# Routing three batches of attention output in two lanes, with the rank in planned free steps of its PSUM bank

## The chip, the cores and the metric

The kernel runs on one core of one Trainium2 chip. The metric is the device time of one execution in microseconds (us), lower is better. Five engines work in parallel, each through its own instructions in order: PE (TensorE, matmuls; PEld are its weight loads), DVE (VectorE), ACT (ScalarE), POOL (GpSimd) and SP (SyncE, which here only issues DMAs). ACT and POOL also issue DMAs from their own queues.

## The reference

Three layers follow each other: attention with a threshold, a mixture of eight experts with one expert for each token, and a dense layer with softplus.

```python
# attention: batch 4, heads 8, seq 576, head_dim 64
scores = scale * q @ k.T
scores = where(scores >= max(scores) - tau, scores, -1e9)
attn = exp(scores - max(scores)); attn /= attn.sum() + 1e-9
x = (attn @ v) -> tokens x 512                    # 2304 x 512
# experts: 8, 512 -> 1024 -> 512
logits = (x / |x|) @ (emb / |emb|).T / tau
idx = argmax(logits); gate = softmax(logits)[idx]
out[n] = gate[n] * (relu(x[n] @ w1[idx[n]]) @ w2[idx[n]])
# dense: 512 -> 2048 -> 512
y = softplus(out @ w_in) @ w_out
```

## The kernel before, in words

The program is written under a manual schedule: each engine runs its instructions in the order in which the code emits them. It has three stages: attention (phase A, to about 380 us), experts (phase B, to about 660 us) and the dense layer (phase C, to the end).

Phase A works on 144 chunks (`NCH`), 36 for each of four batches: a chunk is 128 query rows of one head (or 64 rows of two heads). A step of the loop emits one chunk of scores on PE (`emit_s`, L314), their maximum and mask on DVE (`emit_max` L324, `emit_mask` L329), the exponentials on ACT (`emit_exp`, L340) and, some steps behind, the split of older chunks into two half floats (`emit_hi` on ACT, L354; `emit_lo` on POOL, tile `PST`), their transposition (by DMA from SP's queue, and a part on PE into the tile `T`, which ACT or DVE copy out in `emit_land`, L387 and L389) and the product with V (`emit_pv`, L412), ten steps behind the scores. DVE then scales the product into the rows `xs` (L428 to L438). What is emitted where is set by a list of (time, function): `at(n, ...)` puts a function near the end of step n, `soon(t, ...)` at a time t. Step n starts at the DVE instruction L324 of chunk n.

After the list comes the drain, whose order is written out as words (`DRAIN`): a letter and a number name a chunk function, or let one of the lanes take a step (z is lane 0, a lane 1, b lane 2).

Beside the chunks each step does a part of two slower jobs:

- **V of the next batch.** It is loaded in four pieces (`load_v`, from ACT's queue, into the one buffer `vst`), its greatest magnitude is found (`max_v`, ACT, L238), this is turned and spread by PE (`prep_v0`, `prep_vb`) and scaled on DVE (`prep_v1`, `prep_vc`, L256 to L277), and then V is scaled and rounded on ACT (`prep_v2`, L286 and L288, one head every second step) with the remainder on POOL (`prep_v3`, tile `vl`). `V0, VD, VM, VMD, VP` say at which step of a batch these parts stand.
- **Routing of the batch before.** For each 128 tokens, `route_sq` sums squares (ACT, L452), `route_t` transposes the rows on PE into a PSUM tile `xt_ps` (L460), `route_x` copies it out on ACT (L470), `route_l` makes the logits on PE (L481) and `route_c` copies them on DVE (L486). When the five pieces of a batch are there, generators do the rest, one small instruction at each half step: `route_norm` (the norm's reciprocal), `route_pick` (greatest logit, choice `eq`, `im`, one-hot `oh`), `route_gate` (softmax weight), `route_rank` (each token's place in its expert's bucket: matmuls L565 into a PSUM tile `rk_ps`, then `eq` L569 and `ix` L577 on DVE, the running counts `runs` on POOL) and `route_out` (five indirect DMAs on POOL, L615, that scatter the rows `xs` to the DRAM table `bucket`).

The PSUM tiles of V's chain (`vx_ps`, `vb_ps`), `xt_ps`, `lg_ps` and `rk_ps` are all cut from one pool `pr` with the tag `xt` and one buffer: a single bank. Whoever comes next on PE waits until the last user's copy has been read. The list `held` marks, while the program is being emitted, that a logits tile or a tile of V's chain is in use; `route_t` does not enter itself there.

Phase B starts with `counts` (tokens for each expert), loads of weights and of the first expert's rows from `bucket` (`load_x`, SP's queue, behind all scatters), 40 small matmuls, a branch on the overflow of a bucket (`overflow`), 40 more matmuls (`warm_up`, L1092), the gate's product with the rows (`gate_x`) and their transposition (`turn_first`, tile `x_ps`, L951) before the first expert matmul (L980).

Of the kernel before, what the change touches and what calls it, by code (L numbers as in the profile page):

```python
# [20 lines left out]
B, H, S, HD = 4, 8, 576, 64  # L21
# [13 lines left out]
PLAG = 5  # L35
WARMB, WARMC = 40, 40
TX0, TX = 4, 2
RKY, RKZ, VM, VMD = 2, 3, 17, 2
RKN, SUN, SU0 = 4, 0, 12
SBB, GQB, PTB = 6, 4, 4  # L40
LGL, LGZ, RNL, RSZ = 4, 3, 2, 3
C0 = NCH - 18
# [1 line left out]
OUTY = 2  # L44
EVA, EVH = 0, 0
DRAIN = """P8 g0 a1 z1 l2 a1 H2 a1 a1 H1 D3 a1 t5 P7 P6 a1 t4 D1 u5 L2 t3 a1 P5 c2 z1 p0 b1 V9 b1 a1 u4 a1 u3 P4 b1 t1 V5 b1 z1 b1 u1 t2 a1 u2 a1 z1 b1 z1 z1 a1 P3 r3 b1 b1 a1 x3 q3 b1 P2 V3 a1 b1 a1 g1 d1 d1 a1 P1 V1 l3 d1 r4 g2 d1 c3 q4 p1 d1 x4 d1 e1 f1 d1 e1 l4 f1 d1 e1 f1 e1 f1 d1 f1 e1 c4 z1 d1 e1 p2 h1 d1 e1 f1 d1 e1 f1 h1 a1 d1 e1 f1 h1 d1 f1 h1 f1 h1 f1 h1 d1 e1 d1 e1 e1 f1 h1 h1 e1 f1 d1 e1 f1 d1 e1 h1 d1 f1 f1 h1 e1 d1 d1 h1 d1 h1 e1 d1 e1 f1 h1 d1 e1 f1 h1 h1 e1 f1 f1 h1 d1 f1 h1 d1 e1 f1 e1 e1 f1 d1 f1 d1 e1 d1 h1 e1 h1 b1 h1 a1 z1 b1 z1 f1 b1 h1 a1 z1 b1 e1 e1 e1 b1 a1 a1 a1 d1 e1 b1 e1 d1 d1 e1 d1 e1 d1 d1 e1 d1 d1"""
QK0, QKD, V0, VD, VP, VS, Z0, ZD = 12, 7, 14, 2, 26, 2, 12, 1.5
DQ, DZ, VG = (0, 0, 0, 0), 1, 1
VA, VC, VE, VF = (1, 2, 3, 4), (3, 5), (5, 6, 7, 8, 9, 10, 11, 12), 1
NRING, L2LAG, CLAG, RAWB = 4, 2, 3, 3  # L50
# [11 lines left out]
def attention_moe_moe_kernel(ctx: ExitStack, tc, qT, kT, v, tau, emb, moe_tau, w1, w2, wi, wo, out):  # L62
# [121 lines left out]
    def phase_a():  # L184
        with ExitStack() as es:
# [359 lines left out]
            def route_rank(b, t0, t1, eq, oh, shift):  # L545
                T, R = t1 - t0, 64 if t0 == 4 else 128
                if T > 1:
                    sm1 = ry.tile([128, NE], F32, tag="sm1", name="sm1")[0:R]
                    dve.tensor_reduce(out=sm1, in_=oh.rearrange("p t e -> p e t"), axis=AX.X, op=ALU.add)
                    yield  # L550
                else:
                    shift()
                    IX[b, t0] = None
                    sm1 = oh[:, 0]
                    yield
                if b == B - 1 and t0 > 0:
                    pt = ps.tile([128, 2, 512], F32, tag="S", name="rk_ps")
                else:
                    while held:
                        yield  # L560
                    pt = pr.tile([128, 1, 512], F32, tag="xt", name="rk_ps")
                for t in range(T):
                    mms = ([(tri[0:R], oh[:, t]), (ones, runs)] + [(ones[0:R], oh[:, u]) for u in range(t)])
                    for z, (l, r) in enumerate(mms):
                        pe.matmul(pt[:, 0, t * NE:(t + 1) * NE], l, r, start=(z == 0), stop=(z == len(mms) - 1))  # L565
                if b == B - 1:
                    dve.tensor_tensor(out=runs[0:R], in0=runs[0:R], in1=sm1, op=ALU.add)
                    yield
                dve.tensor_tensor(out=eq, in0=pt[0:R, 0, 0:T * NE].rearrange("p (t e) -> p t e", t=T), in1=oh,  # L569
                                  op=ALU.mult)  # L570
                yield
                if b < B - 1:
                    combine(pool, runs[0:R], runs[0:R], sm1, ALU.add)
                    yield
                ix = sm.tile([128, 5], I32, tag="ix", name="ix")[0:R, 0:T]
                with nc.allow_low_precision(reason="whole numbers under 2**24"):
                    dve.tensor_reduce(out=ix, in_=eq, axis=AX.X, op=ALU.add)  # L577
                yield
                IX[b, t0] = ix
# [42 lines left out]
                    for _ in range(OUTY):  # L622
                        yield

            def route(b, t0, t1):
                yield from route_norm(b, t0, t1)
                for _ in range(RKN):
                    yield
                picked = yield from route_pick(b, t0, t1)
                yield from route_gate(b, t0, t1)  # L630
                for _ in range(RKY if b < B - 1 else 0):
                    yield
                yield from route_rank(b, t0, t1, *picked)
                yield from route_out(b, t0, t1)

            def route_p(b, t0, t1):
                picked = yield from route_pick(b, t0, t1)
                yield from route_rank(b, t0, t1, *picked)

            def route_g(b, t0, t1):  # L640
                yield from route_norm(b, t0, t1)
                while (b, t0) not in IX:
                    yield
                yield from route_gate(b, t0, t1)
                while IX[b, t0] is None:
                    yield
                for _ in route_out(b, t0, t1):
                    pass

            UT = {}  # L650

# [19 lines left out]
            def step_lane(k, n=1):  # L671
                q = lanes[k]
                for _ in range(n):
                    while q:
                        try:
# [2 lines left out]
                        except StopIteration:  # L678
                            q.pop(0)

            def step_tiny(n=0):
                for k in range(len(lanes)):
                    step_lane(k, TS if n > NFAST else 1)

# [34 lines left out]
            def at(n, fn, *a):  # L719
                work.setdefault(n, []).append((fn, a))  # L720
# [3 lines left out]
            def soon(t, fn, *a):  # L724
                late.append((t, fn, a))
# [26 lines left out]
            at(SU0, push, setup(em, ident16, pr, rt))  # L752
            for b in range(B):
                s0 = 36 * b
                for j in range(4):
                    at(s0 + QK0 + QKD * j, load_k, b + 1, j)
                    at(s0 + QK0 + QKD * j + 3, scale_k, b + 1, j)
                    at(s0 + QK0 + QKD * j + 2, load_q, b + 1, j)
                    at(s0 + V0 + VD * j, load_v, b + 1, 2 * j)
                    at(s0 + VM + VMD * j, max_v, b + 1, j)  # L760
                soon(s0 + VP + 0.05, prep_v0, b + 1)
                soon(s0 + VP + 1.18, prep_v1, b + 1)
                soon(s0 + VP + 2.85, prep_vb, b + 1)
                soon(s0 + VP + 3.18, prep_vc, b + 1)
                for i in range(0, 8, VN):
                    at(s0 + VP + 4 + VS * i, prep_v2, b + 1, i, VN)
                    at(s0 + VP + 5 + VS * i, prep_v3, b + 1, i, VN)
                    if (i + VN) % 2 == 0:
                        at(s0 + VP + 4 + VG + VS * i, prep_v4, b + 1, i + VN - 2, 2)
                for t in range(5 if b < B - 1 else 2):  # L770
                    s1 = pv_step[s0 + 8 * t + (7 if t < 4 else 3)] + (3 if b < B - 1 else RSZ)
                    at(s1, route_sq, b, t)
                    at(s1 + 1, route_t, b, t)
                    at(s1 + 1, route_x, b, t)
                    lg = LGL if b < B - 1 else LGZ
                    at(s1 + lg, route_l, b, t)
                    soon(s1 + lg + 1.19, route_c, b, t)
                    if t == 4:
                        at(s1 + RNL, push, route(b, 0, 5))
            for fn in (route_sq, route_t, route_x):  # L780
                at(NCH - 2, fn, B - 1, 2)
            for e in range(NE):
# [570 lines left out]
```

## Time and profile before

| | |
|---|---|
| median of 3 runs | 1097.32 us (1090.73 to 1097.51) |
| profiled execution | 1093.78 us, of which its span is 1092.1 us |
| PE / PEld busy | 978.2 / 834.6 us (90% / 76% of the span) |
| DVE / ACT / POOL busy | 713.8 / 609.2 / 560.6 us |
| mean granted TensorE clock | 0.959 |

The page of the profile gives, for one execution, each engine's busy time, the span in 40 slices, and the chain that ended last. A view of windows gives the same by stretch. A timeline lists instructions by start, with the idle time of that engine just before each and what released it. Busy shares are averages over stages with different limits, so each stage is read for itself.

### The profile page before, as it was taken

To read this page: it belongs to the slowest core of one execution; us is meant where nothing else is said; L and a number is where in the kernel's file an instruction comes from. 1 tells how busy PE (TensorE), PEld (TensorE's weight loads), DVE (VectorE), ACT (ScalarE), POOL (GpSimd) and SP (SyncE) were. 2 spreads that over 40 slices of the span, in tenths; PEclk is the share of its full clock that TensorE was granted. 3 is DMA by queue.
4 is the path that set the end of the run, shared out by engine and by line. 5 is a ranking of instruction groups with operands and counts; after the bars stand their busy time and mean duration, and the time that the engine had idled before them with its cause. 6 is when DMAs were issued, how large, how long until landed. Compare 5 with 4: busy or idle time off the path is not lost. (4 is left out here: it accounts for less than half of the span.)

```text
span 1092.1 us, 18861 instructions
## 1 busy us (share of the span) xinstructions
PE 978.2 (90%) x7110; PEld 834.6 (76%) x7110; DVE 713.8 (65%) x1393; ACT 609.2 (56%) x1070; POOL 560.6 (51%) x477
## 2 busy tenths in 40 slices
PE   7777986988888779989999988987999999999997
PEld 5566765766666769988998887765888888889896
DVE  7878897788689637666776658888433533444543
ACT  6769888788778525444444434445444544454543
POOL 4646665766766425544654431221655565565652
PEclk8889999899899879999999999999999999999999
DMA  6789997697667466978778775220200110010000
GB/s 161 157 152 180 181 222 133 135 187 127 138 105 112 134 223 194 220 157 192 208 231 196 167 180 135 91 87 20 77 1 1 30 39 1 29 40 1 29 1 30
DMA packets 181956, 128.39 MB, mean 118 GB/s; under 512 B 128856, under 2 KB 154456, under 8 KB 181856
## 3 DMA queue, kind: packets, MB, share of 16 engines
q1 hardware_dynamic: 162912, 99.84, 42.4%
q10 hardware_dynamic: 16032, 17.78, 6.1%
q0 software_dynamic: 2912, 9.48, 2.3%
q8 instruction: 58, 0.95, 0.4%
q14 instruction: 42, 0.34, 0.1%
HBM read 75.05 MB, written 20.01 MB: 87 GB/s over the span
## 5 line engine op out<-in xcount | busy, mean ns | idle before, releaser
L84 POOL TENSOR_TENSOR PST<-E,PST 128x1152 f16<-128x1152 f32 (+1 forms) x74 | 169.1, 2287 | 117.4 <-ACT PST L354 80.3
L1233 PE MATMUL a<-wo,g 128*128 128x512 f32 x864 | 218.4, 399 | 9.5 <-DVE g L84 9.5
L1205 PE MATMUL ch_ps<-cxt,wi 128*128 128x512 f32 (+1 forms) x960 | 214.3, 372 | 5.2 <-DVE cxt L84 3.2
L1205 PEld LDWEIGHTS ch_ps<-cxt,wi 128*128 128x128 f32 x960 | 177.2, 189 | 34.4 <-DVE cxt L84 3.5
L1233 PEld LDWEIGHTS a<-wo,g 128*128 128x128 f32 x864 | 162.1, 189 | 49.2 <-DVE g L84 14.0
L84 POOL TENSOR_TENSOR t<-e,t 128x512 f32<-128x512 f32 (+1 forms) x78 | 92.6, 1187 | 203.5 <-DVE t L1217 203.5
L314 PE MATMUL S<-k,qz 128*128 128x288 f32 x512 | 166.2, 451 | 8.7 <-ACT k L216 3.5
L324 DVE TENSOR_SCALAR_CACHE_REDUCE Sb<-S,tau_s 128x576 f32<-128x576 f32 x144 | 116.7, 810 | 46.5 <-PE S L314 36.8
L980 PE MATMUL h_ps<-xt,w 128*128 128x320 f32 x768 | 133.2, 323 | 12.7 <-ACT w L839 8.3
L84 POOL TENSOR_TENSOR w<-st,w 128x1024 fp32r<-128x1024 f32 x30 | 74.5, 2482 | 121.8 <-ACT w L839 121.6
L1217 DVE TENSOR_SCALAR t<-e 128x512 f32<-128x512 f32 (+1 forms) x80 | 33.6, 421 | 157.5 <-ACT e L1215 157.5
L980 PEld LDWEIGHTS h_ps<-xt,w 128*128 128x128 f32 x768 | 118.5, 195 | 18.2 <-ACT w L839 9.9
L1214 ACT ACTIVATE e<-ch_ps 128x512 f32<-128x512 f32 (+1 forms) x80 | 44.1, 551 | 154.1 <-PE ch_ps L1205 154.1
L996 PE MATMUL y<-h,w 128*128 128x320 f32 x768 | 123.0, 310 | 0.0
L329 DVE SCALAR_TENSOR_TENSOR Sb<-S,th,Sb 128x576 f32<-128x576 f32 x144 | 117.8, 818 | 5.1
L996 PEld LDWEIGHTS y<-h,w 128*128 128x128 f32 x768 | 115.7, 189 | 0.0
L314 PEld LDWEIGHTS S<-k,qz 128*128 128x128 f32 x512 | 93.8, 204 | 27.8 <-issue 5.0
L412 PEld LDWEIGHTS <-PT 128*128 128x128 f16 (+1 forms) x2240 | 87.2, 103 | 28.8 <-DMA PT<-PST 10.3
L340 ACT ACTIVATE E<-Sb,nb 128x576 f32<-128x576 f32 x144 | 103.8, 768 | 6.4 <-ACT nb L337 0.4
L412 PE MATMUL pv<-vh,PT 128*128 128x65 f16 (+1 forms) x1440 | 96.0, 197 | 10.8 <-DMA PT<-PST 7.5
L84 POOL TENSOR_TENSOR g<-g,t 128x512 f32<-128x512 f32 (+1 forms) x62 | 87.0, 1404 | 4.9
L839 ACT ACTIVATE w<-st 128x1024 fp32r<-128x1024 f32 x64 | 67.3, 1053 | 31.9 <-DMA st<-in_w 29.6
(185 smaller groups left out, 1377.1 us busy)
## 6 DMA issues: line engine op xcount, KB each, us to landing
st<-in_w SPq DMA_DIRECT2D x64, 512.0 KB, 4.8
raw<-in_wi SPq DMA_DIRECT2D x16, 512.0 KB, 4.2
raw<-in_wo SPq DMA_DIRECT2D x16, 512.0 KB, 5.4
bucket<-qz SPq DMA_DIRECT2D x32, 161.2 KB, 5.8
yT<-y ACTq DMA_DIRECT2D x7, 640.0 KB, 11.9
vst<-in_v ACTq DMA_DIRECT2D x12, 320.0 KB, 4.8
xr<-bucket SPq DMA_DIRECT2D x7, 516.0 KB, 6.3
k<-in_kT ACTq DMA_DIRECT2D x12, 288.0 KB, 4.0
```

Of the source, the lines that this page charges most:

```text
L84: eng.tensor_tensor(out=out, in0=a, in1=b, op=op)
L314: pe.matmul(st[:, f, 0:HALF], q[:, h // 2, o:o + 128], k[:, h // 2, fs])
L324: dve.tensor_scalar(out=Sb[n], in0=St[n][:, :, 0:HALF], scalar1=tau_s[:, 0:1], scalar2=None, op0=ALU.subtract, op1=ALU.max, accum_out=TH[g ...
L329: dve.scalar_tensor_tensor(out=Sb[n], in0=St.pop(n)[:, :, 0:HALF], scalar=TH[g][:, j:j + 1], in1=Sb[n], op0=ALU.is_lt, op1=ALU.subtract)
L340: act.activation(out=Et[g][:, i].rearrange("p (f k) -> p f k", f=2), in_=Sb.pop(g * GS + i), func=ACTF.Exp, scale=-SCALE, bias=nb[:, i:i + 1])
L412: pe.matmul(oo, l, r, start=(z == 0), stop=(z == len(mms) - 1))
L839: act.activation(out=hi, in_=src, func=ACTF.Copy)
L980: pe.matmul(hps[:, 0:CAP], a[:, c, 128 * (f % 2):128 * (f % 2) + 128], b[:, c], start=(z == 0), stop=(z == 11))
L996: pe.matmul(Y[e][c][:, 0:CAP], a[:, f % 2, 128 * c:128 * c + 128], b, start=(f == 0 and z == 0), stop=(f == 7 and z == 2))
L1205: pe.matmul(h, a[:, r:r + 128], x[:, c, 0:n], start=(z == 0), stop=(z == 11))
L1214: act.activation(out=e, in_=h, func=ACTF.Abs)
L1233: pe.matmul(A[b][t], a[:, 128 * t:128 * t + 128], x, start=(f == 0 and z == 0), stop=(f == 15 and z == 2))
```

## The change

For the first three batches the routing is no longer one generator in lane 0. Norm, gate and scatter run in lane 1 (`route_g`), choice and rank in lane 2 (`route_p`), as it already was for the last batch; the waits between them by counts of empty steps (`RKN`, `RKY`) go. The rank is emitted only in a step n where neither n nor n+1 stands in a set `taken`, which is filled with the steps of V's chain, of `route_t` and of `route_l`; and it enters itself in `held` until DVE has read its tile. V of the third and fourth batch is loaded, measured and scaled earlier in the batch (`VSLOT`: chain from step 18 of the batch, where it was 26); V of the second batch stays.

```diff
--- before.py
+++ after.py
@@ -35,8 +35,7 @@
 PLAG = 5
 WARMB, WARMC = 40, 40
 TX0, TX = 4, 2
-RKY, RKZ, VM, VMD = 2, 3, 17, 2
-RKN, SUN, SU0 = 4, 0, 12
+SUN, SU0 = 0, 12
 SBB, GQB, PTB = 6, 4, 4
 LGL, LGZ, RNL, RSZ = 4, 3, 2, 3
 C0 = NCH - 18
@@ -44,7 +43,8 @@
 OUTY = 2
 EVA, EVH = 0, 0
...
-QK0, QKD, V0, VD, VP, VS, Z0, ZD = 12, 7, 14, 2, 26, 2, 12, 1.5
+QK0, QKD, VS, Z0, ZD = 12, 7, 2, 12, 1.5
+VSLOT = (14, 2, 17, 2, 26), (10, 1, 13, 1, 18)
 DQ, DZ, VG = (0, 0, 0, 0), 1, 1
 VA, VC, VE, VF = (1, 2, 3, 4), (3, 5), (5, 6, 7, 8, 9, 10, 11, 12), 1
 NRING, L2LAG, CLAG, RAWB = 4, 2, 3, 3
@@ -556,8 +556,9 @@
                 if b == B - 1 and t0 > 0:
                     pt = ps.tile([128, 2, 512], F32, tag="S", name="rk_ps")
                 else:
-                    while held:
+                    while b < B - 1 and (held or {now[0], now[0] + 1} & taken):
                         yield
+                    held.extend([1] * (b < B - 1))
                     pt = pr.tile([128, 1, 512], F32, tag="xt", name="rk_ps")
                 for t in range(T):
                     mms = ([(tri[0:R], oh[:, t]), (ones, runs)] + [(ones[0:R], oh[:, u]) for u in range(t)])
@@ -565,7 +566,9 @@
                         pe.matmul(pt[:, 0, t * NE:(t + 1) * NE], l, r, start=(z == 0), stop=(z == len(mms) - 1))
                 if b == B - 1:
                     dve.tensor_tensor(out=runs[0:R], in0=runs[0:R], in1=sm1, op=ALU.add)
-                    yield
+                yield
+                if b < B - 1:
+                    held.pop()
                 dve.tensor_tensor(out=eq, in0=pt[0:R, 0, 0:T * NE].rearrange("p (t e) -> p t e", t=T), in1=oh,
                                   op=ALU.mult)
                 yield
@@ -622,17 +625,6 @@
                     for _ in range(OUTY):
                         yield
 
-            def route(b, t0, t1):
-                yield from route_norm(b, t0, t1)
-                for _ in range(RKN):
-                    yield
-                picked = yield from route_pick(b, t0, t1)
-                yield from route_gate(b, t0, t1)
-                for _ in range(RKY if b < B - 1 else 0):
-                    yield
-                yield from route_rank(b, t0, t1, *picked)
-                yield from route_out(b, t0, t1)
-
             def route_p(b, t0, t1):
                 picked = yield from route_pick(b, t0, t1)
                 yield from route_rank(b, t0, t1, *picked)
@@ -645,7 +637,8 @@
                 while IX[b, t0] is None:
                     yield
                 for _ in route_out(b, t0, t1):
-                    pass
+                    if b < B - 1:
+                        yield
 
             UT = {}
 
@@ -678,7 +671,10 @@
                         except StopIteration:
                             q.pop(0)
 
+            now, taken = [0], set()
+
             def step_tiny(n=0):
+                now[0] = n
                 for k in range(len(lanes)):
                     step_lane(k, TS if n > NFAST else 1)
 
@@ -752,6 +748,8 @@
             at(SU0, push, setup(em, ident16, pr, rt))
             for b in range(B):
                 s0 = 36 * b
+                V0, VD, VM, VMD, VP = VSLOT[b > 0]
+                taken.update(range(s0 + VP, s0 + VP + 4))
                 for j in range(4):
                     at(s0 + QK0 + QKD * j, load_k, b + 1, j)
                     at(s0 + QK0 + QKD * j + 3, scale_k, b + 1, j)
@@ -771,12 +769,15 @@
                     s1 = pv_step[s0 + 8 * t + (7 if t < 4 else 3)] + (3 if b < B - 1 else RSZ)
                     at(s1, route_sq, b, t)
                     at(s1 + 1, route_t, b, t)
+                    taken.update((s1 + 1, s1 + 2))
                     at(s1 + 1, route_x, b, t)
                     lg = LGL if b < B - 1 else LGZ
                     at(s1 + lg, route_l, b, t)
+                    taken.update((s1 + lg, s1 + lg + 1))
                     soon(s1 + lg + 1.19, route_c, b, t)
                     if t == 4:
-                        at(s1 + RNL, push, route(b, 0, 5))
+                        at(s1 + RNL, push, route_g(b, 0, 5), 1)
+                        at(s1 + lg + 2, push, route_p(b, 0, 5), 2)
             for fn in (route_sq, route_t, route_x):
                 at(NCH - 2, fn, B - 1, 2)
             for e in range(NE):
```

On PE, in step 73 before (batch 0's rank, the first of the three; `pv` is the product with V, `tri` and `ones` constant matrices):

```order
L412 MATMUL pv_2613<-vh_187,PT 128x65
L460 MATMUL xt_ps<-ident,xs 128x128 x4
L565 LDWEIGHTS tri
L565 MATMUL rk_ps<-oh,tri 128x8
L565 LDWEIGHTS ones
L565 MATMUL rk_ps<-runs,ones 128x8
```

and now, in step 62:

```order
L412 MATMUL pv_2208<-vh_187,PT 128x65
L314 MATMUL S<-k,qz_120 128x288 x2
L566 LDWEIGHTS tri
L566 MATMUL rk_ps<-oh,tri 128x8
L566 LDWEIGHTS ones
L566 MATMUL rk_ps<-runs,ones 128x8
```

The rank's 20 matmuls stood right behind the transposition that fills the same bank; they now stand behind a chunk of scores, two steps after `route_l`. Batch 1's move in the same way from step 109 to step 98, and batch 2's from the drain to step 133.

On DVE, in step 73 before:

```order
L324 TENSOR_SCALAR Sb,th<-S,tau_s 128x576
L329 SCALAR_TENSOR_TENSOR Sb<-S,th,Sb 128x576
L549 TENSOR_REDUCE sm_2714<-oh 128x8
L569 TENSOR_TENSOR eq<-rk_ps,oh 128x40
L324 TENSOR_SCALAR Sb,th<-S,tau_s 128x576
```

and now, in step 62:

```order
L324 TENSOR_SCALAR Sb,th<-S,tau_s 128x576
L329 SCALAR_TENSOR_TENSOR Sb<-S,th,Sb 128x576
L428 SCALAR_TENSOR_TENSOR rd<-pv_2208,vma 128x4
L432 RECIPROCAL rd<-rd 128x4
L438 TENSOR_TENSOR xs<-pv_2208,rd 128x256
L572 TENSOR_TENSOR eq<-rk_ps,oh 128x40
```

DVE reads the rank's tile in the same step in which PE fills it, as before, now behind the scaling of a product.

On POOL, at the end of the loop and in the drain before (the last seven `PST` are chunks 134 to 140 and 142; `bucket` rows are scatters):

```order
L84 TENSOR_TENSOR PST<-E,PST 128x2x576
L84 TENSOR_TENSOR PST<-E,PST 128x576 x2
L602 TENSOR_SCALAR gt<-gt 128x5
L84 TENSOR_TENSOR PST<-E,PST 128x576 x4
L84 TENSOR_TENSOR runs<-runs,sm_5576 128x8
L615 DMA bucket<-xs,ix 18432x516
```

and now:

```order
L618 DMA bucket<-xs,ix 18432x516
L621 MEMSET pad 1x1
L84 TENSOR_TENSOR PST<-E,PST 128x2x576
L618 DMA bucket<-xs,ix 18432x516
L621 MEMSET pad 1x1
L84 TENSOR_TENSOR PST<-E,PST 128x576
L618 DMA bucket<-xs,ix 18432x516
L621 MEMSET pad 1x1
L84 TENSOR_TENSOR PST<-E,PST 128x576
L618 DMA bucket<-xs,ix 18432x516
L621 MEMSET pad 1x1
L84 TENSOR_TENSOR PST<-E,PST 128x576 x4
```

Batch 2's five scatters (two stand ahead of the first `PST` row, one of them is shown) moved from the drain, where ten stood in a row, to between the last `PST`; five are left behind them.

## Rows read from the trace of the kernel before

**Rows 1.** Windows view, 10 us: busy time by engine, granted clock, DMA.
```profile
190.00:200.00 10.00, 7.16 (x80) 5.69 (x80) 4.29 (x12) 4.56 (x8) 4.04 (x6) 0.66 0.52 100
```

**Rows 2.** Timeline of DVE around step 73: start, us, work, idle before.
```profile
186.25 0.81 DVE L324 TENSOR_SCALAR_CACHE_REDUCE Sb<-S,tau_s 128x576 f32<-128x576 f32 x1
...
193.55 0.20 DVE L569 TENSOR_TENSOR eq<-rk_ps,oh 128x40 f32<-128x40 f32 x1 [5.50 <-PE rk_ps L565]
195.77 0.82 DVE L324 TENSOR_SCALAR_CACHE_REDUCE Sb<-S,tau_s 128x576 f32<-128x576 f32 x1 [2.02 <-PE S L314]
```

**Rows 3.** Timeline of PE around step 73.
```profile
186.18 0.63 PE L460 MATMUL xt_ps<-ident,xs 128*128 128x128 f32 x4
192.84 0.17 PE L565 MATMUL rk_ps<-oh,tri 128*128 128x8 f16 x1 [6.02 <-ACT xt L470]
```

**Rows 4.** Timeline of ACT around step 73.
```profile
190.57 0.68 ACT L387 ACTIVATE PT<-T 128x640 f16<-128x640 f16 x1
...
192.21 0.58 ACT L470 ACTIVATE xt<-xt_ps 128x512 f32<-128x512 f32 x1
...
199.06 0.20 ACT L337 ACTIVATE nb<-th 128x2 f32<-128x2 f32 x1 [5.32 <-DVE Sb L324]
```

**Rows 5.** Timeline of DVE around step 109.
```profile
274.33 0.81 DVE L324 TENSOR_SCALAR_CACHE_REDUCE Sb<-S,tau_s 128x576 f32<-128x576 f32 x1
...
283.29 0.82 DVE L324 TENSOR_SCALAR_CACHE_REDUCE Sb<-S,tau_s 128x576 f32<-128x576 f32 x1 [2.02 <-PE S L314]
```

**Rows 6.** Timeline of DVE, steps 81 and 82.
```profile
210.85 0.80 DVE L324 TENSOR_SCALAR_CACHE_REDUCE Sb<-S,tau_s 128x576 f32<-128x576 f32 x1
...
213.55 0.82 DVE L324 TENSOR_SCALAR_CACHE_REDUCE Sb<-S,tau_s 128x576 f32<-128x576 f32 x1 [1.04 <-ACT E L340]
```

**Rows 7.** Timeline of DVE, steps 62 to 66.
```profile
159.17 0.82 DVE L324 TENSOR_SCALAR_CACHE_REDUCE Sb<-S,tau_s 128x576 f32<-128x576 f32 x1
...
166.11 1.54 DVE L539 TENSOR_TENSOR oh<-iota,im 128x40 f16<-128x40 f32 x1
...
172.59 0.82 DVE L324 TENSOR_SCALAR_CACHE_REDUCE Sb<-S,tau_s 128x576 f32<-128x576 f32 x1 [3.04 <-PE S L314]
```

**Rows 8.** Timeline of POOL beside step 64.
```profile
165.22 2.37 POOL L84 TENSOR_TENSOR PST<-E,PST 128x1152 f16<-128x1152 f32 x1 [1.13 <-ACT PST L354]
```

**Rows 9.** Timeline of DVE, steps 26 and 30.
```profile
77.88 0.81 DVE L324 TENSOR_SCALAR_CACHE_REDUCE Sb<-S,tau_s 128x576 f32<-128x576 f32 x1
...
88.37 0.82 DVE L324 TENSOR_SCALAR_CACHE_REDUCE Sb<-S,tau_s 128x576 f32<-128x576 f32 x1 [1.82 <-PE S L314]
```

**Rows 10.** Waits of SP's queue, 100 to 350 us: total, times, longest.
```profile
SPq L365 <- DMA k<-in_kT: 4.8, 1, 4.8
```

**Rows 11.** Timeline of POOL, last steps of the loop.
```profile
346.36 4.85 POOL L84 TENSOR_TENSOR PST<-E,PST 128x1152 f16<-128x1152 f32 x3 [2.02 <-ACT PST L354]
```

**Rows 12.** Timeline of PE, last steps of the loop.
```profile
354.75 0.20 PE L412 MATMUL pv<-vh,PT 128*128 128x65 f16 x1 [2.14 <-DMA PT<-PST]
```

**Rows 13.** Timeline of POOL, scatters after the loop (ten in all).
```profile
372.01 1.11 POOL L615 DMA_INDIRECT bucket<-xs,ix  x1 [3.43 <-DVE nrm L90]
...
379.65 0.90 POOL L615 DMA_INDIRECT bucket<-xs,ix  x1 [0.24 <-DVE off L1025]
...
383.62 1.97 POOL L615 DMA_INDIRECT bucket<-xs,ix  x1 [0.22 <-issue]
...
385.90 0.90 POOL L615 DMA_INDIRECT bucket<-xs,ix  x1 [0.22 <-issue]
```

**Rows 14.** Timeline of SP's queue, start of the expert stage.
```profile
389.74 0.82 SPq L930 DMA_DIRECT2D xr<-bucket  x2
```

**Rows 15.** Timeline of PE, start of the expert stage.
```profile
386.74 4.45 PE L1092 MATMUL warm<-ones 128*128 128x128 f16 x40 [4.27 <-DVEq L1073]
393.49 0.63 PE L951 MATMUL x_ps<-ident,xr 128*128 128x128 f32 x4 [2.31 <-DVE xr L947]
...
396.48 5.80 PE L980 MATMUL h_ps<-xt,w 128*128 128x320 f32 x20 [0.21 <-ACT xt L839]
```

## The prediction

> **What bounds the kernel now.** The change moves nothing behind the hand-over to phase B, so only phase A and the hand-over are in play. In phase A no engine is full, so I timed the steps one by one, from one L324 on DVE to the next, and looked for those that stand out. The reader is to see two. Step 73 lasts from 186.25 to 195.77 us, 9.52 us [rows 2]; step 109 from 274.33 to 283.29, 8.96 us [rows 5]. These are the steps in which the ranks of batches 0 and 1 stand.
>
> PE's timeline says why. The transposition into `xt_ps` starts at 186.18, and behind it the rank's first matmul waits 6.02 us for the bank, until ACT's copy of `xt_ps`; that copy starts at 192.21 only, since ACT works through its own queue in order and has scores, V and the sum of squares ahead of it [rows 3, 4]. DVE has asked for the rank's result meanwhile: it stands 5.50 us for it and 2.02 us more for the next scores, which PE issues behind the rank [rows 2]. The granted clock of the window from 190 us averages 0.66 of full speed [rows 1]: a part of it ran at 1.2 GHz instead of 2.4. PE's idle time came first, the low clock with and after it; both lie inside the 9.52 us.
>
> **The change, part by part.** The sum is made against the profiled execution, 1093.78 us.
>
> *The two stalls.* Step 81 holds the same parts (a transposition into the bank, its copy on ACT, one head of V) without a rank: 213.55 - 210.85 = 2.70 us [rows 6]. Against it the ranks cost 9.52 - 2.70 = 6.82 and 8.96 - 2.70 = 6.26 us, 13.1 together. With the rank in step 62 (98), two steps behind `route_l` and three ahead of the next `route_t`, PE meets a bank that DVE has just read, and DVE needs its own turn there anyway. What is late next is ACT. In step 73 it is behind: it copies `T` out from 190.57 to 191.25 [rows 4], and PE wants `T` again in step 75, which without the stall comes at some 189.3 us (DVE would begin step 74 at 186.25 + 2.70 = 188.95, and PE runs somewhat ahead of it; an estimate). So up to 1.9 us of each stall can come back as a wait for `T`; some of it is slack between PE and DVE, and ACT has no head of V to scale after step 72 any more. I take 0.9 each, nearer the middle than either end: 13.1 - 1.8 = 11.3, ends 9.3 and 13.1.
>
> *The rank's own work.* It doesn't vanish: 20 small matmuls (from 192.84 to DVE's read at 193.55, 0.7 us [rows 2, 3]) and three small DVE instructions (0.20 us for L569 [rows 2]), so 0.4 us of DVE's path for each of the three ranks, the third of which comes out of the drain: -1.2, ends -1.8 and -0.6.
>
> *V's chain, loads and scale, eight steps earlier.* Routing's transpositions and logits come every eight steps, so the chain meets the same neighbours on the bank. What differs is the choice: in steps 62 to 65 the chain stood beside `im` and `oh`, and the four steps took 172.59 - 159.17 = 13.42 us, with one `oh` of 1.54 us [rows 7]. The same steps of batch 0, with no routing beside them, took 88.37 - 77.88 = 10.49 [rows 9]. Now the choice ends two steps behind the chain, but its first instructions and the norm's reciprocal stand inside. Of the 2.9 us I take 0.7, for two batches 1.4; ends 0 and 5.2. V's pieces are now loaded one step apart instead of two, beside K, Q and the zero fills; the trace shows no wait of ACT for a piece of V, and one of SP's transpositions for K, 4.8 us [rows 10]. I take -0.5, ends 0 and -2. V's scale costs ACT the same sixteen instructions, in steps 58 to 72 instead of 66 to 80.
>
> That `oh` took 1.54 us while POOL was subtracting for `PST`, from 165.22 to 167.59, and ended with it [rows 7, 8]. The Trainium skill, SBUF — State Buffer, section Who interferes with whom, says that a DVE instruction with two inputs in SBUF contends with a GpSimd instruction that reads SBUF, and that whoever starts second is blocked until the other ends. The row agrees. By the page the `oh` of the new place is as exposed as the old one, since POOL subtracts in every second step, and the saving at V's chain may be nil: the sum would give 1081.8 in place of 1080.4.
>
> *The scatters at the end of the loop.* From 379.65 to 383.62 three scatters follow each other, 1.32 us each with memset and gap [rows 13]. Two now stand ahead of the `PST` of chunks 134 and 135, where POOL had 2.02 us idle [rows 11]: 2.64 - 2.02 = 0.6 us late, and PE waits for just that transposition (2.14 us [rows 12]), so 0.6 us reach the path. The three behind it delay chunks 136 to 138; their products came without a wait, and POOL stands idle again further on. I take -0.6 for all, ends 0 and -3. The low end takes in that a scatter can last longer than these: one took 1.97 [rows 13].
>
> *The hand-over.* Ten scatters stood in a row behind the drain; the last starts at 385.90, and its landing lets SP load the first expert's rows at 389.74 [rows 13, 14]. Five are left. The one at 379.65 is released by DVE's last routing work and stays, so the last scatter and the loads come 385.90 - 379.65 = 6.25 us earlier. Not all of that counts: PE waits at the branch until 386.74 and then runs 40 matmuls for 4.45 us, to 391.19 [rows 15], and neither hangs on a scatter. The transpositions began at 393.49, so 2.3 us come from there; twelve transpositions at 0.63 for four are 1.9 of the 2.99 us from there to the first expert matmul at 396.48, and of the 1.1 that is left, waits for later rows, I count 0.7. I take 3.0, ends 2.3 and 3.8 (the rank's matmuls that leave the drain add up to 0.8).
>
> Sum: 11.3 - 1.2 + 1.4 - 0.5 - 0.6 + 3.0 = 13.4 us, so 1093.8 - 13.4 = 1080.4. All low ends give 9.3 - 1.8 + 0 - 2 - 3 + 2.3 = 4.8, all high ends 13.1 - 0.6 + 5.2 + 3.8 = 21.5: 1089 and 1072. The profiled execution lies 3.5 us under the median of the runs and 3.1 above their lowest; runs of the new kernel may sit as far to either side. I forecast **1081 us**.
>
> **The rivals.** *ACT is what paces these steps.* Then PE's wait only moves. For it: ACT begins the copy over five microseconds after PE has filled the bank. Against: after the stall ACT stands idle 5.32 us [rows 4], time that the loop gave it and that it didn't need. If ACT sets the pace, the eight steps from the stall's end at 195.77 [rows 2] to step 82 at 213.55 [rows 6] show it: 2.22 us each with V's scale beside them. Sixteen such steps take 35.6 us, where steps 66 to 81 took 213.55 - 172.59 = 41.0. The stall would then give 5.4 us at most, and the wait for `T` at its full 1.9 off that: two times 3.5, 4.3 us less than the forecast: 1085, or 1087 with late scatters.
>
> *Slower: the loads choke the transpositions.* V's four pieces, K and Q go out within five steps, and SP's queue, which issues the transpositions, already waited 4.8 us once behind a load of K [rows 10]. Each batch has a store of about ten steps between a chunk's scores and its product. If SP falls behind by more than what is left of it, PE stops as it did at 354.75, in the middle of the loop. At 9 us for each of the two batches, the size of the steps that now stand out, that is 1080.4 + 18 = 1098 us. It decides from a point at which transpositions land later than their product is due; in the loop's middle PE showed no such wait.
>
> *The change doesn't do what it says*: the free steps are free in the plan, yet PE waits there for the logits' copy or DVE for the rank, as it did. The plan counts steps, not time. Two thirds of the 13.1 us in the new places, 8.7 back: 1089.
>
> **How the numbers follow.** Forecast 0.72, ACT's pace 0.14, loads 0.05, no real freedom 0.09. The range takes in the forecast's own bounds, ACT's pace and the third rival: 1072 to 1090. A measurement of this kernel can tell about 1% (11 us) from no change. Below 1086.3 us lie the forecast, but for its low end, and half of ACT's pace: 0.74 faster. Slower by over 1% would take 1108 us, which only loads worse than priced reach: 0.04. The rest, 0.22, is within 1%.
>
> **What the profile after would show.** Right: steps 73 and 109 last 2.5 to 4.5 us; the rank's matmuls stand in steps 62, 98 and 133 with waits under 1 us; no window at these places has a granted clock near 0.66; a short wait of PE for ACT's copy of `T` remains in step 75; the last scatter starts about 6 us closer to the branch, and PE goes from its second 40 matmuls to the transpositions without 2.31 us of idle. Wrong: a step over 6 us anywhere between 54 and 82, PE waiting for `PT` in mid-loop, or ACT waiting for V. What would upset the forecast most is a new stall in steps 54 to 57, where V's chain and the start of the choice now share DVE.

## The result, and the profile after

The changed kernel took 1083.87 us (median of four executions, 1081.11 to 1085.16), the kernel before 1097.41 beside it: a ratio of 0.9883, 95% interval 0.9841 to 0.9925. Two later comparisons gave 0.9897 and 0.9901. The profiled execution took 1081.11 us, its span 1079.3, where before it was 1093.78 and 1092.1. The forecast was 1081 for the runs and 1080.4 for the profiled execution. The sum came out near; one of its terms, V's loads, lies far outside its ends, and one stretch that it left out moved. All lengths "before" below are from one profile, so differences of a microsecond or two may be its own spread.

The two long steps are gone. The timeline of DVE after, steps 73 and 109, answers to [rows 2, 5]:

```profile
190.60 0.81 DVE L324 TENSOR_SCALAR_CACHE_REDUCE Sb<-S,tau_s 128x576 f32<-128x576 f32 x1
...
193.62 0.82 DVE L324 TENSOR_SCALAR_CACHE_REDUCE Sb<-S,tau_s 128x576 f32<-128x576 f32 x1 [1.36 <-PE S L314]
...
273.75 0.82 DVE L324 TENSOR_SCALAR_CACHE_REDUCE Sb<-S,tau_s 128x576 f32<-128x576 f32 x1 [0.69 <-ACT vh L288]
...
275.90 0.82 DVE L324 TENSOR_SCALAR_CACHE_REDUCE Sb<-S,tau_s 128x576 f32<-128x576 f32 x1 [0.47 <-PE S L314]
```

Step 73 lasts 3.02 us, step 109 2.15. The timeline of PE after, the rank in step 62 and the transposition of step 73, answers to [rows 3]:

```profile
166.57 0.17 PE L566 MATMUL rk_ps<-oh,tri 128*128 128x8 f16 x1 [0.36 <-DVE lg L486]
...
191.17 0.45 PE L379 MATMUL T<-ident,PST 128*128 128x128 f16 x5 [0.82 <-POOL PST L84]
191.89 0.63 PE L460 MATMUL xt_ps<-ident,xs 128*128 128x128 f32 x4
```

The rank waits 0.36 us for the logits' copy in place of 6.02 us for ACT. And ACT is still late with its own copy, by its timeline after [rows 4]:

```profile
196.00 0.58 ACT L470 ACTIVATE xt<-xt_ps 128x512 f32<-128x512 f32 x1
```

Four microseconds lie between the transposition's start and this copy, as six did before. Nothing on PE needs the bank meanwhile, so they cost nothing. The window after from 190 us has the full clock [rows 1]; the second row below is of the window from 140 us:

```profile
190.00:200.00 10.00, 9.06 (x115) 7.18 (x114) 8.43 (x18) 9.15 (x16) 7.56 (x6) 1.00 0.86 155
...
140.00:145.00 5.00, 3.73 (x26) 3.04 (x27) 0.00 (x0) 1.42 (x4) 3.49 (x9) 0.50 1.24 196
```

There the low clock has turned up again, and with it a new long step, 52 of the loop: 7.59 us, in the last 5.92 of which DVE does nothing. The timelines of DVE and of PE after:

```profile
137.82 0.81 DVE L324 TENSOR_SCALAR_CACHE_REDUCE Sb<-S,tau_s 128x576 f32<-128x576 f32 x1
...
145.41 0.82 DVE L324 TENSOR_SCALAR_CACHE_REDUCE Sb<-S,tau_s 128x576 f32<-128x576 f32 x1 [5.92 <-PE S L314]
```

```profile
134.60 1.21 PE L314 MATMUL S<-k,qz 128*128 128x288 f32 x4
141.26 0.23 PE L412 MATMUL pv<-vh,PT 128*128 128x65 f16 x1 [5.45 <-DMA PT<-PST]
...
143.09 2.29 PE L314 MATMUL S<-k,qz 128*128 128x288 f32 x4
```

PE stops for a transposed piece, and the next scores take 2.29 us in place of 1.21, at 1.2 GHz (0.50 of full speed in that window). The transpositions come from SP's queue; its timeline after:

```profile
125.18 2.46 SPq L365 DMA_TRANSPOSE PT<-PST  x1
128.56 0.59 SPq L181 DMA_DIRECT2D bucket<-qz  x1
132.18 2.41 SPq L365 DMA_TRANSPOSE PT<-PST  x1
134.64 0.80 SPq L181 DMA_DIRECT2D bucket<-qz  x1
135.59 4.43 SPq L365 DMA_TRANSPOSE PT<-PST  x1
```

And SP's own waits from 115 to 150 us:

```profile
SPq L365 <- DMA vst<-in_v: 2.9, 1, 2.9
SPq L365 <- DMA vh<-vh: 1.0, 1, 1.0
```

The transposition that PE wants had its input by 127.17 and was issued at 132.18, and it needs nothing of V. What it waits for is a completion counter: the instruction streams of the compiled program show that the DMAs issued by SP and ACT share eight counters, and one that inherits a counter waits until its last user has landed. ACT's first two measures of V and SP's transposition, in the changed kernel's streams (the waits of the instructions just ahead are put with the transposition's own):

```
207 L238 ACTIVATE vl_183,vmx<-vst 128x640 [waits DMAHW4_49]
211 L238 ACTIVATE vl_183,vmx<-vst 128x640 [waits DMAHW5_49]
64 L365 DMA_TRANSPOSE PT<-PST 128x13x128 [waits DMAHW4_49,DMAHW5_49,PE_49,Pool_49]
```

The counter that matters is `DMAHW5_49`: the transposition and ACT's second measure wait for the same value of it, 192, which V's second piece brings (on `DMAHW4_49` the transposition waits for an older value, 176). In the trace that counter reaches its value at 132.10 us, and the transposition goes out at 132.18. SP's 2.9 us are thus about half of PE's 5.45; the rest lies in the landing, some 9 us from 132.18 to PE's restart at 141.26, where the median over the loop is 5.2.

At the end of the loop five scatters stand between or just ahead of the last `PST` and five behind the loop, by the timeline of POOL after, which answers to [rows 11, 13]:

```profile
336.92 1.11 POOL L618 DMA_INDIRECT bucket<-xs,ix  x1 [0.16 <-DVE xs L438]
...
346.89 0.91 POOL L618 DMA_INDIRECT bucket<-xs,ix  x1 [0.17 <-issue]
...
372.87 0.90 POOL L618 DMA_INDIRECT bucket<-xs,ix  x1 [0.22 <-issue]
```

PE, in the last steps and at the hand-over, by its timeline after [rows 12, 15]:

```profile
347.52 0.20 PE L412 MATMUL pv<-vh,PT 128*128 128x65 f16 x1 [2.38 <-DMA PT<-PST]
...
380.37 4.45 PE L1093 MATMUL warm<-ones 128*128 128x128 f16 x40 [4.33 <-DVEq L1074]
384.61 1.94 PE L952 MATMUL x_ps<-ident,xr 128*128 128x128 f32 x12
386.89 4.16 PE L981 MATMUL h_ps<-xt,w 128*128 128x320 f32 x24 [0.34 <-ACT xt L840]
...
651.09 4.16 PE L1206 MATMUL ch_ps<-cxt,wi 128*128 128x512 f32 x17 [0.67 <-ACTq L1149]
```

The 2.31 us of idle ahead of the transpositions are gone. The first expert matmul comes 9.6 us earlier than before, the first of the dense layer (the last row) 12.8 us. The same instruction in the timeline of PE before:

```profile
663.86 4.38 PE L1205 MATMUL ch_ps<-cxt,wi 128*128 128x512 f32 x18 [0.66 <-ACTq L1148]
```

### The profile page after: what moved, and what is told of

The parts are those of the page before. It is cut to its first block, busy times and chain, and to the rows that moved or that the text cites. A ratio compares the mean times of both kernels' runs of the same rounds, so it can differ in the third digit from the quotient of the medians.

```text
span 1079.3 us, 18861 instructions
## 1 busy us (share of the span) xinstructions
PE 976.4 (90%) x7110; PEld 832.1 (77%) x7110; DVE 710.0 (66%) x1393; ACT 609.2 (56%) x1070; POOL 558.8 (52%) x477
## 5 line engine op out<-in xcount | busy, mean ns | idle before, releaser
L324 DVE TENSOR_SCALAR_CACHE_REDUCE Sb<-S,tau_s 128x576 f32<-128x576 f32 x144 | 116.6, 810 | 52.0 <-PE S L314 37.4
L981 PE MATMUL h_ps<-xt,w 128*128 128x320 f32 x768 | 131.1, 319 | 11.3 <-ACT w L840 6.6
L981 PEld LDWEIGHTS h_ps<-xt,w 128*128 128x128 f32 x768 | 116.1, 191 | 17.2 <-ACT w L840 8.2
```

The lines of the kernel that those rows point to most:

```text
L324: dve.tensor_scalar(out=Sb[n], in0=St[n][:, :, 0:HALF], scalar1=tau_s[:, 0:1], scalar2=None, op0=ALU.subtract, op1=ALU.max, accum_out=TH[g ...
L981: pe.matmul(hps[:, 0:CAP], a[:, c, 128 * (f % 2):128 * (f % 2) + 128], b[:, c], start=(z == 0), stop=(z == 11))
```

## The experiments

Lengths of steps are worked out from the starts of L324 on DVE, as in the prediction. "The loop" below is steps 36 to 142: 256.6 us before, 250.7 after. Ratios are to runs of the kernel before on the same chip: 1088.32 us (median) beside `again`, `rank_back`, `v_back` and `v_alone`, 1090.04 beside `v_pool`, `fills_early`, `scatter_late` and `rank_only`, 1092.25 beside `v_mid`, `kq_later`, `v_back2` and `again2`.

**The changed kernel again** (`again`; no edit).

> The changed kernel once more, for a second profile on another run. Theory A (the stall in step 52 and the 3 us of phase B belong to the kernel): the time is 1081 to 1085 us, step 52 lasts 6 to 8 us again, with PE waiting over 4 us for PT, and the first matmul of the dense layer comes 12 to 13 us earlier than in the profile of before. Rival B (both are chance of one execution): step 52 lasts under 3 us, or the expert stage has its old length, and the profiled execution lies some 6 us lower or 3 us higher.

1076.49 us, ratio 0.9897 (0.9852 to 0.9942). That is 4.5 us under the range expected, but the kernel before was 9 us faster beside it too. The loop took 249.9 us and step 52 7.44, so the new stall belongs to the kernel. The expert stage doesn't; the timeline of PE:

```profile
386.73 4.16 PE L981 MATMUL h_ps<-xt,w 128*128 128x320 f32 x24 [0.34 <-ACT xt L840]
...
643.11 5.28 PE L1206 MATMUL ch_ps<-cxt,wi 128*128 128x512 f32 x22 [0.67 <-ACTq L1149]
```

256.4 us from one to the other, where the first profile of the same kernel had 264.2 and that of before 267.4. Each theory was right in one half. Over all profiles of this study, with the same code in this stage, it lasted 255.1 to 267.4 us, and those taken beside each other lie closer (255.1 to 259.7 for `v_pool` and its three neighbours, 262.7 to 265.9 for `v_mid` and its three). So 3.2 of the 12.8 us between the first two profiles show nothing about the change.

**The ranks back behind the transposition** (`rank_back`).

```diff
-while b < B - 1 and (held or {now[0], now[0] + 1} & taken):
+while b < B - 1 and (held or (behind[0] != 36 * (b + 2) + 1 if b < 2 else {now[0], now[0] + 1} & taken)):
...
```

`behind` holds the step of the last `route_t`, so the ranks of batches 0 and 1 stand in steps 73 and 109.

> The changed kernel with the ranks of batches 0 and 1 back behind the transposition of steps 73 and 109; V's slot and the lanes stay as changed. Theory A (the order on the one bank made the stalls): steps 73 and 109 last 8 to 9.5 us again, PE waits 5 to 6 us there, and the kernel is 11 to 13 us slower than the changed one, near before. Rival B (ACT was late there because V's scale stood beside it, and that has moved): the two steps last under 5 us, and the kernel is 0 to 5 us slower than the changed one.

1089.53 us, ratio 1.0009 (0.9976 to 1.0042): the whole gain is gone. The timelines of PE and of DVE, step 73:

```profile
196.18 0.17 PE L567 MATMUL rk_ps<-oh,tri 128*128 128x8 f16 x1 [5.66 <-ACT xt L471]
```
```profile
199.11 0.82 DVE L324 TENSOR_SCALAR_CACHE_REDUCE Sb<-S,tau_s 128x576 f32<-128x576 f32 x1 [7.76 <-PE S L314]
```

Steps 73 and 109 last 9.44 and 9.86 us. It is the order on the bank that made the stalls; that most of V's scale has left their neighbourhood doesn't help.

**V in its old steps** (`v_back`, and `v_back2` beside `again2` on one chip).

```diff
-VSLOT = (14, 2, 17, 2, 26), (10, 1, 13, 1, 18)
+VSLOT = (14, 2, 17, 2, 26), (14, 2, 17, 2, 26)
```

> The changed kernel with V's loads, measure and chain of all batches in the old steps; lanes and the rank's rule stay, so the ranks go to the next free steps, 70, 106 and 141. Theory A (V's new slot saves some 4 to 5 us at each chain and pays 6 in step 52 and 3.6 in steps 91 and 93): step 52 lasts under 2.5 us, steps 63 to 65 and 99 to 101 last 9 to 11 us again, some scatters of batch 2 fall into the drain again (+1 to +3), and the time is within 4 us of the changed kernel. Rival B (the moved V is what makes the gain): 1090 us or more.

> The changed kernel with V of all batches in the old steps, timed beside the changed one on one chip. By the two profiles so far (steps 36 to 143: 245.1 us with V in the old steps, 249.9 and 250.7 in the new) it is 4 to 8 us faster than the changed kernel, ratio to before 0.981 to 0.985. If V's new slot costs nothing, the two ratios agree within 0.2%.

> The changed kernel, timed beside the last one: ratio to before 0.988 to 0.990, step 52 at 6 to 8 us, ranks in steps 62, 98 and 133. If step 52's stall were chance, it is under 3 us in this profile.

`v_back`: 1073.58 us, ratio 0.9836 (0.9773 to 0.9899). `v_back2`: 1076.76, 0.9857 (0.9832 to 0.9882). `again2`: 1082.11, 0.9901 (0.9868 to 0.9933). The version with V left where it was is the faster one in both pairs, by 0.6 and 0.4%. The intervals of a pair overlap, so the ratios alone don't settle it; the loop does: it took 245.1 and 243.4 us, where the three profiles of the changed kernel have 249.9 to 251.4. The timeline of DVE, step 52 of `v_back`, and PE's waits from 100 to 350 us:

```profile
145.56 0.81 DVE L324 TENSOR_SCALAR_CACHE_REDUCE Sb<-S,tau_s 128x576 f32<-128x576 f32 x1
...
147.14 0.81 DVE L324 TENSOR_SCALAR_CACHE_REDUCE Sb<-S,tau_s 128x576 f32<-128x576 f32 x1
```
```profile
PE pv L412 <- DMA PT<-PST: 5.3, 2, 3.1
```

Step 52 lasts 1.58 us there, steps 73 and 109 1.69. Steps 63 to 65 last 8.07 us, not the 9 to 11 expected: with the choice in a lane of its own the old steps of the chain are cheaper too (11.09 before). In `again2` the stall is spread over steps 50 (6.90 us) and 52 (4.63), and SP's transpositions wait 3.8 us for one of V's copies (`vh`) besides 1.7 for its loads.

**V's move alone** (`v_alone`): the kernel before with `VSLOT` as changed.

> The kernel before with V's new slot alone: ranks in steps 73 and 109, routing in one lane. Theory A (the bank's order makes the stalls): steps 73 and 109 last over 7 us as before, step 52 lasts 6 to 8 us, the chain's steps 63 to 65 and 99 to 101 are shorter by 4 to 5 us each, and the time is within 4 us of before. Rival B (V's scale beside the transposition made ACT late): steps 73 and 109 last under 5 us, and the kernel is 6 to 13 us faster than before.

1089.98 us, ratio 1.0011 (0.9979 to 1.0043). PE's waits from 100 to 350 us:

```profile
PE pv L413 <- DMA PT<-PST: 13.9, 6, 4.9
PE rk_ps L566 <- ACT xt L471: 11.1, 2, 5.7
```

Steps 73 and 109 last 8.95 and 9.96 us, step 52 7.03. The chain's old steps are 4.3 and 4.8 us shorter, as expected, and that is paid back at the loads, at the chain's new place, and in step 66, which lasts 6.56 us where it had 2.34: there PE stops 3.5 us for a piece that SP sent late, as the transposition ahead of it had waited 5.2 us for a load of Q.

**The rank's rule alone** (`rank_only`): the kernel before with `taken`, `now` and the entry in `held`, in one lane.

> The kernel before with the rank's rule alone (free steps, entry in the list of users): one lane, V in its old steps; the ranks of batches 0 and 1 stand in steps 78 and 114, batch 2's in the drain. Theory A (the order on the bank made the stalls, and nothing else of the change is needed for that gain): steps 73, 78, 109 and 114 last under 4 us each, the kernel is 11 to 14 us faster than before, as fast as the changed one. Rival B (norm, choice and rank in two lanes carry part of the gain): under 8 us.

1082.6 us, ratio 0.9928 (0.9898 to 0.9959): 7.8 us, less than expected. Steps 73 and 109 last 1.71 and 1.73 us, but step 86 lasts 6.84 where it had 3.12. The timelines of POOL (the last scatter of batch 0) and of DVE:

```profile
215.69 0.90 POOL L618 DMA_INDIRECT bucket<-xs,ix  x1 [0.22 <-issue]
```
```profile
222.47 0.42 DVE L438 TENSOR_TENSOR xs<-pv,rd 128x256 f32<-128x256 f32 x1 [2.37 <-DMA bucket<-xs,ix]
222.81 2.25 DVE L113 TENSOR_SCALAR nrm<-ss 128x5 uint32<-128x5 uint32 x1
```

With the rank in step 78 the scatters go out so late that DVE waits for their landing before it may write the next `xs` (two buffers). The two lanes bring the rank to step 62, or 70 with V in its old steps, and keep that away. Rival B holds: the lanes carry part of the gain. Its bound of 8 us lies inside the interval (4.5 to 11 us), but `v_back`, the same with two lanes, gains 16 to 18. Not all is accounted for: by the first expert matmul (393.45) this profile is 3.0 us ahead of the one before, and where the rest of the 7.8 lies isn't known.

**Who chokes the transpositions**: four kernels. V's loads of batches 1 and 2 from POOL's queue (`v_pool`); the zero fills in steps 6 to 44 (`fills_early`); V's loads two steps apart with the chain two steps later (`v_mid`); K and Q of batch 1 later (`kq_later`).

```diff
+at(s0 + V0 + VD * j, load_v, b + 1, 2 * j, pool if b > 0 else act)   # v_pool
+QK0, QKD, VS, Z0, ZD = 12, 7, 2, 6, 1.25                             # fills_early
+VSLOT = (14, 2, 17, 2, 26), (10, 2, 13, 2, 20)                       # v_mid
+QKS, VS, Z0, ZD = ((12, 7), (16, 6), (12, 7), (12, 7)), 2, 12, 1.5   # kq_later
```

> The changed kernel with V's eight loads of batches 1 and 2 issued from POOL's queue, not ACT's: same bytes, same steps, but outside the eight completion counters that the DMAs of SP and ACT take in turn. Theory A (a transposition that inherits the counter of a V load has to wait until that load has landed, and SP's queue stands behind it): SP shows no wait for vst, step 52 lasts under 4 us. Rival B (the bytes of V, K, Q and the zero fills crowd the DMA engines, so that transpositions land late): step 52 lasts 6 to 8 us as before, and the transpositions there take 9 us to land.

> The changed kernel with its 32 zero fills in steps 6 to 44 instead of 12 to 58, so that none stands beside V's loads of batch 1. Both theories of step 52 let its stall go (under 3 us), the kernel is some 5 us faster than the changed one, 1070 to 1073 beside its 1076, unless the denser fills stall the transpositions of batch 0: then the steps 14 to 36 are longer by as much. If V's loads alone did it, step 52 stays at 6 to 8 us.

> The changed kernel with V's loads of batches 1 and 2 two steps apart again (steps 10, 12, 14, 16 of the batch), each piece measured three steps behind its load, and the chain from step 20. The chain then has a transposition of the routing inside, which costs some 1 to 3 us per batch. Theory A (four V loads in four steps make the loads and the transpositions behind them late): step 52 lasts under 3 us, the wait of PE for PT between 46 and 54 is under 1 us, and steps 36 to 143 take 246 to 250 us where the changed kernel took 250 to 251. Rival B (what counts is that V is loaded beside the zero fills and K, Q at all): a step between 50 and 58 of 5 us or more remains.

> The changed kernel with batch 1's loads of K and Q four steps later and six apart (K in 52, 58, 64, 70, Q two steps behind each), so that in steps 46 to 50 V's loads stand beside zero fills alone. If V's loads and the fills are enough to choke the transpositions: step 52 lasts 6 to 8 us. If it takes K and Q too: step 52 lasts under 3 us, and no step from 50 to 60 lasts over 5 us.

`v_pool` (1072.46 us, one execution): step 52 lasts 1.59 us, but step 54 6.79. SP's waits from 115 to 160 us, and the timeline of PE:

```profile
SPq L365 <- DMA qz<-in_qT: 7.5, 2, 7.2
```
```profile
144.65 0.27 PE L250 MATMUL vx_ps<-ident,vmx 128*4 128x128 f32 x1 [4.16 <-ACT vl L238]
```

Now a transposition waits 7.2 us for a load of Q, and V itself lands so late that its measure holds up the chain. So both theories hold a part: the loads land late where many stand together (`v_mid`, below, with the same loads further apart, shows no wait of SP for a load there), and the counters are the way by which that reaches a transposition.

`fills_early` (1079.55 us, 0.9892, interval 0.9853 to 0.993; the loop 256.9 us): its condition did not come about. SP ran behind, so that the last fills slid to 135 us and still stood beside V's loads, step 40 became 6.88 us and step 52 kept 6.69. (Step 40 isn't the edit's alone: it took 5.66 us in `scatter_late`, which leaves the fills where they were, and 2.14 to 3.36 in the three profiles of the changed kernel.) SP's waits from 115 to 150 us:

```profile
SPq L181 <- DMA vh<-vh: 4.4, 1, 4.4
SPq L365 <- DMA k<-in_kT: 3.3, 1, 3.3
```

`kq_later` (1079.25 us, one execution): step 52 lasts 2.15 us, so in this profile it takes K and Q too; steps 46 to 53 are still 2.6 us longer than before. Its loop is no shorter, 250.7 us: steps 62 to 66 take 14.4 us in place of 11.9, with the moved loads beside them.

`v_mid` (1091.27 us, 0.9986, interval 0.9959 to 1.0013): no stall in steps 46 to 53, 17.8 us as before, and SP waits for no load there. But V is measured too late for the chain; PE's waits from 100 to 350 us:

```profile
PE T L379 <- ACT PT L387: 9.3, 7, 2.8
PE vx_ps L250 <- ACT vl L238: 6.5, 2, 3.3
```

Steps 56 and 57 last 5.1 us each, rival B's sign by its length, but at V's measure and not at a transposed piece. The loop takes 253.9. Its profiled execution, 1082.85 us, is among the lowest of its ten, so the profile shows 3 us of some 9 that it loses against the changed kernel; where the rest goes stays open.

**Batch 2's scatters behind the loop** (`scatter_late`).

```diff
+if b == B - 2:
+    while now[0] < NCH - 1:
+        yield
+    push(route_out(b, t0, t1), 0)
+    return
```

> The changed kernel with batch 2's five scatters put off behind the loop, as they were. The forecast's sum (-0.6 at the end of the loop, +3.0 at the hand-over): steps 126 to 143 get 0 to 3 us shorter, and from the last step to the first expert matmul it takes some 3 us longer, 38 to 40 us in place of 36. Rival (the scatters in the loop cost nothing and the hand-over gains nothing from them): both stretches as in the changed kernel within 1 us.

1080.37 us, one execution. Steps 126 to 142 take 38.1 us (40.2, 39.1 and 39.0 in the three profiles of the changed kernel, 37.3 before). From the last step to the first expert matmul it takes 36.7 us, as long as in the changed kernel (35.9, 36.7, 36.2), where before took 39.6. The timeline of POOL:

```profile
355.80 1.11 POOL L618 DMA_INDIRECT bucket<-xs,ix  x1 [0.15 <-DVE nrm L87]
...
361.61 0.96 POOL L618 DMA_INDIRECT bucket<-xs,ix  x1 [0.22 <-issue]
```

With their rank done in step 133, four go out early behind the loop and delay nothing. So for the hand-over the scatters need not stand in the loop; it seems enough that their rank has left the drain: 39.6, 39.3 and 38.1 us in the three kernels with that rank in the drain (before, `rank_only`, `v_alone`), 34.0 to 36.9 in the eleven profiles of the others. The three are also those with one lane, and no run parts the two.

## Why the prediction was right

Its mechanism held: the bank's order made the two stalls, and moving the ranks takes them away (`rank_back`). Its sum came out by luck, an offset of errors. Against the first expert matmul, 9.6 us of the 13.4 that it put there were gained; the other 3.2 of the measured 12.8 are the expert stage's spread. By its steps, before against after in the first two profiles:

| term | forecast (ends) | steps | measured |
|---|---|---|---|
| two stalls | +11.3 (9.3 to 13.1) | 73, 109 | +13.3 |
| rank's own work | -1.2 (-1.8 to -0.6) | 62, 98, 133, 134 | -1.0 |
| V's chain | +1.4 (0 to 5.2) | 54 to 61, 63 to 65, 90 to 97, 99 to 101 | +3.9 |
| V's loads | -0.5 (-2 to 0) | 46 to 53 | -6.8 |
| scatters, end of loop | -0.6 (-3 to 0) | 126 to 132, 135 to 142 | -2.0 |
| hand-over | +3.0 (2.3 to 3.8) | last step to first expert matmul | +3.7 |
| not in the sum | | 102 to 108: -3.0; all others: +1.5 | -1.5 |

*The stalls.* The two steps alone gave 13.3 us. In step 75, where the prediction looked for the give-back, none came: PE doesn't wait there for ACT's copy of `T`, and the step lasts 1.98 us as before. But something came back close by, where PE waits for a `PST` of POOL (step 71 is 0.8 us longer, steps 107 and 108 together 2.7; the table has this in its last row). The rival *ACT is what paces these steps* priced sixteen steps at 35.6 us. Steps 66 to 81 went from 41.0 to 34.9 us and steps 102 to 117 from 41.6 to 36.5: 11.2 us together (10.5 and 9.8 in the two other profiles), against 11.3 in the sum. In `v_back`, `v_back2` and `rank_only`, which have V's scale beside these steps as before had, both stretches take 35.4 to 35.6 us, and PE does wait 1.5 us for ACT's copy of `T` in step 75. So the rival's pace is about what these steps take, and no run excludes that ACT sets it; its time came out late as it took 1.9 us more off each stall.

*V's loads: the step that failed.* The prediction read "no wait of ACT for a piece of V" [rows 10] as slack and took -0.5. It had named the mechanism, as the rival *Slower*, with SP falling behind and PE stopping in mid-loop, and put it at 9 us for each of two batches with a chance of 0.05. It came true in one batch: steps 46 to 53 lose 6.8 us, and 6.3 and 7.0 in the two other profiles. PE waiting for `PT` in mid-loop was one of the prediction's own signs of being wrong. In batch 2 no step from 82 to 89 lasts longer than before. The view before from which [rows 10] come has one row more that bears on it, a zero fill on SP's queue that waited for a load of V:

```profile
SPq L181 <- DMA vst<-in_v: 2.5, 1, 2.5
```

So SP's queue had already stood once behind a load of V at the old spacing; that ACT never waited for V said nothing of SP.

*V's chain.* The steps that it left got 3.9 and 5.1 us shorter, the new ones 1.2 and 4.0 longer. The choice that stood beside it [rows 7] moved in both versions, and `v_back` shows that the new lanes alone take 3.0 us off steps 63 to 65. So V's move, which the sum booked at 1.4 - 0.5 = +0.9 us, is a loss of some 5 us as measured.

*Not priced.* In steps 102 to 108 batch 1's scatters meet V's remainder on POOL, and PE waits for a `PST` that POOL has late: 2.17 us in step 107, until 268.56, when POOL's subtraction has ended (268.51). The prediction looked at scatters only at the end of the loop.

*The hand-over.* The size was right, and so was the path: from the start of step 143 the last scatter starts after 21.9 us in place of 29.1, PE's second 40 matmuls after 29.4 in place of 29.9, and PE goes from them to the transpositions without idle, as foretold. What isn't needed for it is the scatters' new place in the loop: `scatter_late` has the gain with the five behind it and its last scatter at 23.9 us.

*The sentence on the page.* By the Trainium skill, SBUF — State Buffer, section Who interferes with whom, the choice's `oh` should have been as exposed in its new place. It took 0.19 us there in batch 0 (1.54 before [rows 7]) and in batch 1 (0.85 before), so nothing was lost by it there; in batch 2 it took 0.78 (0.19 before). V's chain shows a wait of the same kind (last section).

## What to carry to other kernels

Who asks for a shared bank, and in what order, can cost more than all that is done in it: a reader that is four microseconds late is free as long as nobody behind it on the in-order engine wants its buffer. Test the parts of a change apart: here the lanes and the rank's place together earned some 16 us, V's move gave back some 5, and the sum looked right. Slack of a queue read from a quiet stretch doesn't price a denser one; count the DMAs that land per step, and whose counter each one inherits.

## What was not expected of the hardware

- The expert stage, code unchanged, took 255.1 to 267.4 us from profile to profile. ACT's wait in it for weights from DRAM varied too, 16.0 to 29.0 us. Differences under 6 us are better read from the stretch that the change touches.
- A DVE instruction of 4x4 elements took 0.217 us in step 55 and 1.494 us in step 91, where POOL's subtraction ran from 232.60 us to 234.97. DVE's and POOL's timelines after:

```profile
233.50 1.49 DVE L263 TENSOR_SCALAR vmd<-ident,vm 4x4 f32<-4x4 f32 x1
```
```profile
232.60 2.37 POOL L84 TENSOR_TENSOR PST<-E,PST 128x1152 f16<-128x1152 f32 x1 [0.61 <-ACT PST L354]
```

  It ends as soon as POOL has ended. The Trainium skill, SBUF — State Buffer, section Who interferes with whom, says that a `tensor_scalar` can enter a mode that takes the port pair that DVE shares with GpSimd, and that whoever issues first holds the pair for its whole instruction while the other is blocked. The row agrees in its times; whether this instruction ran in such a mode isn't shown. Some 1.3 of the 4.0 us that the chain's new steps lost in batch 2 are this: in `again2` the instruction took 0.292 us, and step 91 lasted 2.87 us in place of 4.06.
